# Attention and a ResMLP block on one core: constant rows on another DMA queue, merged casts of v, the sinks' product issued beside the scores, and a last tile in two column halves

## The chip, the cores and the metric

One NeuronCore of one Trainium2 chip. The metric is the device time of one execution in microseconds (us), as a median of several. TensorE (PE) does the matmuls and transposes, VectorE (DVE), ScalarE (ACT) and GpSimd (POOL) the work on elements, SyncE (SP) only issues DMAs; ScalarE and GpSimd can issue them too. "Granted clock" is the share of its full clock that TensorE was allowed. It is recorded for every run, as a mean over the run, and will turn out to matter here.

## The reference

```python
# q, k, v: (4, 8, 768, 64); n_sink = 4; window = 128
scores = q @ k.T / sqrt(64)
keep = (column < n_sink) | (0 <= row - column < window)
x = softmax(where(keep, scores, -1e9)) @ v       # -> (4, 768, 512)
tok = w_tok @ (alpha1 * x + beta1)               # mixes the 768 positions
u = x + lam * tok
a2 = alpha2 * u + beta2
out = u + lam * (relu(a2 @ w_ch1) @ w_ch2)       # w_ch1: (512, 2048)
```

## The kernel before

The kernel is written as tasks with a priority and a guessed cost. A list scheduler in Python, at build time, turns them into one order of instructions for each engine; the numbers in `TURNS` are seeds of small shuffles of the priorities that were found by trial. Where the scheduler expects TensorE to wait in the start, it puts in filler matmuls (a zero tile times itself, results unused):

```python
    def idle(pt, n):
        for _ in range(n):
            nc.tensor.matmul(pt[:, 0:P], warm, warm, start=True, stop=True)
    plan = Plan(pools, homes, (IDLE, idle, 75.0))
```

In `Plan.emit` they stand ahead of the task that the model expects to come late:

```python
        for t, e, start, stop, idle in self.run(prio):
            if idle:
                self.fill[1](... tile ..., idle[1])     # idle[1] fillers
            ...                                          # allocate buffers
            t.fn(e)                                      # emit the task
```

The three constant rows (lam, alpha1, beta1) are loaded by SyncE's queue into four partitions each, and spread by a shuffle on VectorE:

```python
    def load_row(p, name, tile_, src):
        done["row", name] = add(p, {SP: 500}, lambda e: nc.sync.dma_start(
            tile_.rearrange("(a i) d -> a i d", i=32)[:, 0, :],
            src.unsqueeze(0).to_broadcast([4, DM])), lands=(1, 100))
```

Attention of a tile r of 128 rows is one group of TensorE instructions: the sinks' part first, then the window's:

```python
    def pv(p, b, r, G):
        def mm(e):
            if r >= 2:      # the sinks' columns lie outside the window
                nc.tensor.matmul(po.t, es[b].t[g, (r - 2) * P : (r - 1) * P],
                                 vs[g, 4 * G : 4 * G + 4, :], start=True, stop=False)
            for hl in range(4):
                ...         # window: one or two matmuls a head
```

The result of the MLP of each tile is added and stored whole (512 columns), also in the last tile of all:

```python
                nc.vector.tensor_add(xf, xf, pc.t)
            ... nc.sync.dma_start(out[b, ti * P : (ti + 1) * P, :], ...)
```

The softmax here doesn't subtract the row's maximum and nothing guards it: scores larger than these inputs give would overflow.

## Time and profile before

| | before |
|---|---|
| median of the first 3 runs | 267.05 us (265.82 to 267.19) |
| span of the profiled run, with its time | 263.6 us, 265.35 us |
| first scores of batch 0 start | 13.25 us |
| first token-mixing matmul | 31.62 us |
| first unbroken run of MLP matmuls | 44.38 us |
| last add on VectorE starts | 259.80 us |

The prediction below shows the page's main lines, the waits, the chain and the timeline of the start. One view it does not show is TensorE in single microseconds of the start; one line of it suffices. Columns: stretch, its length, TensorE's busy time with the number of its matmuls, granted clock, DMA share, GB/s.

```profile
10.00:11.00 1.00, 0.00 (x0) 1.00 1.28 198
```

TensorE does nothing from 10 to 11 us: the fillers are in the wrong place, since the cast it waits for (1.62 us of waiting) comes later than the scheduler's model had it. In this run the clock stayed at 1.00. And this run, at 265.35 us, was faster than all three timed ones. Both facts deserved more attention than I gave them.

### The profile page before, as it was taken

The numbers are of one execution on the slowest core, as the hardware profiler recorded it, in microseconds if no ns is written. First come the engines' busy times: TensorE is split into PE (matmuls) and PEld (weight loads), VectorE is DVE, ScalarE is ACT, GpSimd is POOL, SyncE is SP. The second block draws the span as 40 slices with busy tenths as digits, with TensorE's granted clock in tenths as the row PEclk, the third lists the DMA queues.
The fourth block names the chain that finished last, engine by engine and source line by source line (L and its number), as shares of the span: only waits on it lengthen the run. The fifth ranks groups of instructions, "written<-read, shape, count | busy, mean of one in ns | idle before, by whom it ended". The sixth has DMA issues, their size and how long they took to land.

```text
span 263.6 us, 4930 instructions
## 1 busy us (share of the span) xinstructions
PE 254.4 (97%) x1947; PEld 140.3 (53%) x1947; DVE 156.0 (59%) x322; ACT 131.5 (50%) x216; POOL 81.6 (31%) x104
## 2 busy tenths in 40 slices
PE   8699997999999999999999999999999999999994
PEld 7555644765555545555655444556554445564441
DVE  3588996499899835288778327566962451100222
ACT  1499848788764123687740117877500226772000
POOL 8347936332830712333454212111131000000000
PEclk9999999999999999999999999999999999999999
DMA  7999999989937969999658979100012323000222
GB/s 132 195 241 308 295 268 269 371 229 270 210 64 174 221 144 211 183 214 209 120 126 140 249 147 196 44 0 2 1 42 80 80 80 82 0 0 2 80 81 80
DMA packets 85503, 38.49 MB, mean 146 GB/s; under 512 B 73428, under 2 KB 79580, under 8 KB 85480
## 3 DMA queue, kind: packets, MB, share of 16 engines
q1 hardware_dynamic: 81720, 34.90, 55.6%
q0 software_dynamic: 3744, 3.28, 7.9%
q8 instruction: 15, 0.25, 0.4%
q14 instruction: 8, 0.07, 0.1%
q10 hardware_dynamic: 16, 0.00, 0.0%
HBM read 29.65 MB, written 6.29 MB: 136 GB/s over the span
## 4 chain that ended last, share of the span: by engine, by line
PE 88%; DMA 9%; DVE 1%; ACT 0%; issue 0%; SPq 0%; DVEq 0%
PE h L971 32%; PE ch L995 32%; PE tok L891 9%; DMA nat<-in_k_dram 6%; PE S L689 4%; PE pv L773 4%; DMA nat<-in_q_dram 3%; PE S L684 1%; PE pv L766 1%; PE tp L595 1%; PE idle L342 1%; PE tp L592 1%; PE sk L637 1%; PE S_None L689 0%; PE uTp L932 0%; PE vsp_None L656 0%
## 5 line engine op out<-in xcount | busy, mean ns | idle before, releaser
L971 PE MATMUL h<-uT,w1f 128*128 128x384 f16 x512 | 89.3, 326 | 1.3 <-ACT uT L915 1.3
L995 PE MATMUL ch<-w2f,hT 128*128 128x512 f16 x384 | 88.8, 379 | 0.0
L971 PEld LDWEIGHTS <-w1f 128*128 128x128 f16 x512 | 48.3, 98 | 34.1 <-issue 3.6
L977 ACT ACTIVATE hT<-h 128x384 f16<-128x384 f32 x104 | 50.8, 491 | 26.5 <-PE h L971 26.1
L995 PEld LDWEIGHTS <-hT 128*128 128x128 f16 x384 | 36.0, 98 | 40.1 <-issue 0.4
L704 ACT ACTIVATE E<-S 128x1024 f16<-128x1024 f32 (+1 forms) x42 | 41.2, 1004 | 4.2 <-PE S L689 3.0
L1006 DVE TENSOR_TENSOR x<-x,ch 128x512 f32<-128x512 f32 x24 | 16.4, 686 | 44.0 <-PE ch L995 44.0
L813 POOL TENSOR_TENSOR xh<-x,la_b 128x512 f16<-128x512 f32 x18 | 25.3, 1410 | 51.5 <-DVE x L797 46.7
L349 ACT CAST u<-x 128x512 f16<-128x512 f32 x17 | 10.5, 617 | 53.8 <-DVE x L898 52.6
L891 PE MATMUL tok<-xh,wtokT 128*128 128x512 f16 x144 | 34.0, 379 | 0.3 <-DVE x L898 0.2
L898 DVE TENSOR_TENSOR x<-x,tok 128x512 f32<-128x512 f32 x24 | 16.3, 684 | 17.7 <-PE tok L891 17.7
L820 DVE SCALAR_TENSOR_TENSOR x<-lb_b,rsum,x 128x512 f32<-128x512 f32 x24 | 23.6, 1003 | 2.9 <-POOL xh L813 2.9
L891 PEld LDWEIGHTS <-wtokT 128*128 128x128 f16 x144 | 14.0, 98 | 16.8 <-issue 0.7
L351 POOL CAST vf<-vnat 128x512 f16<-128x512 f32 x18 | 12.9, 721 | 28.4 <-DMA vnat<-in_v_dram 17.9
L797 DVE TENSOR_TENSOR x<-pv,rec 128x256 f32<-128x256 f32 x48 | 20.4, 424 | 1.7
L979 DVE TENSOR_SCALAR hT<-h 128x384 f16<-128x384 f32 x24 | 13.2, 554 | 10.6 <-PE h L971 10.3
L773 PEld LDWEIGHTS <-E 128*128 128x128 f16 x328 | 15.3, 98 | 5.7 <-issue 1.4
L773 PE MATMUL pv<-vf,E 128*128 128x65 f16 x328 | 18.0, 194 | 0.0
L713 DVE TENSOR_TENSOR E<-E,maskn 128x1024 f16<-128x1024 f16 x25 | 18.0, 739 | 0.0
L351 POOL CAST n<-nat 128x768 f16<-128x768 f32 x14 | 12.4, 890 | 12.7 <-DMA nat<-in_k_dram 9.5
L351 POOL CAST u<-x 128x512 f16<-128x512 f32 x7 | 4.4, 628 | 33.9 <-DVE x L898 18.7
L689 PE MATMUL S<-qkT 64*128 64x256 f16 (+1 forms) x168 | 13.5, 270 | 0.0
(97 smaller groups left out, 198.1 us busy)
## 6 DMA issues: line engine op xcount, KB each, us to landing
out_dram<-x SPq DMA_DIRECT2D x24, 256.0 KB, 2.1
nat<-in_k_dram SPq DMA_DIRECT2D x13, 384.0 KB, 6.1
nat<-in_q_dram SPq DMA_DIRECT2D x13, 384.0 KB, 6.6
vnat<-in_v_dram SPq DMA_DIRECT2D x18, 256.0 KB, 4.6
wst_w<-in_moe_w_ch_dram SPq DMA_DIRECT2D x8, 512.0 KB, 9.1
wtn<-in_moe_w_tok_dram SPq DMA_DIRECT2D x6, 384.0 KB, 5.2
w1f<-in_moe_w_ch_dram POOLq DMA_DIRECT2D x4, 512.0 KB, 15.0
v<-in_v_dram SPq DMA_DIRECT2D x12, 128.0 KB, 7.6
```

Of the source, the lines that this page charges most:

```text
L351: engine[e].tensor_copy(o, i)
L689: nc.tensor.matmul(pv_[:, e_, i, :], o.t[rows, 2 * hp + 1, j * P : (j + 1) * P], o.t[rows, 2 * hp, j * P : j * P + w], start=not bias, sto ...
L704: nc.scalar.activation(eT.t, pS.t[:, :, 0 : n * w].rearrange("p e (i w) -> p e i w", i=n), AF.Exp, scale=scale)
L713: nc.vector.tensor_mul(ev, ev, m.to_broadcast(list(ev.shape)))
L773: nc.tensor.matmul(po.t[:, hl, :], eT.t[:, e_, off + i, c : c + P], vf[j][:, h, :], start=(r < 2 and n == 0), stop=(n == len(parts) - 1 an ...
L797: nc.vector.tensor_mul(bx.t[:, 4 * G : 4 * G + 4, :], po.t[:, :, 0:D], rec.t.to_broadcast([P, 4, D]))
L813: engine[e].tensor_mul(bh.t, bx.t.rearrange("p h d -> p (h d)"), la1_b)
L820: engine[e].scalar_tensor_tensor(out=xf, in0=lb1_b, scalar=rsum[:, r : r + 1], in1=xf, op0=ALU.mult, op1=ALU.add)
L891: nc.tensor.matmul(pt.t, wtokT[:, si, ti * P : (ti + 1) * P], hs[si].t, start=(si == 0), stop=(si == NR - 1))
L971: nc.tensor.matmul(ph.t, w1f[:, c, fi * P : (fi + 1) * P], bu.t[:, c, chk * NTOK : (chk + 1) * NTOK], start=(c == 0), stop=(c == NC - 1))
L977: nc.scalar.activation(bh.t[:, fi, :], ph.t, AF.Relu)
L995: nc.tensor.matmul(pc.t, bh.t[:, fi, nt * P : (nt + 1) * P], w2f[:, fi, :], start=(fi == 0), stop=(fi == NF - 1))
```

## The change

Its intent: let q and k arrive sooner, make fewer casts, use the array's row halves for the sinks' part of later tiles, and shorten the work after the last matmul. The diff, cut to its core (`TURNS`, the scheduler's constants and its start times also change, so the order of most instructions in the start does too):

```diff
+    for o_, src in ((lam_r, moe_lam), (la1_b, moe_alpha1), (lb1_b, moe_beta1)):
+        nc.scalar.dma_start(
+            o_.rearrange("(a i) d -> a i d", i=32)[:, 0, :], src.unsqueeze(0).to_broadcast([4, DM]))
-    for name, o, src in (("lam", ...), ("a1", ...), ("b1", ...)):
-        load_row(at(), name, o, src)
     def fold_rows():            # multiply first, then spread: one shuffle less
+        for name, key, o, p in (("a1", "la1", la1_b, -987), ("b1", "lb1b", lb1_b, -986)):
+            a = add(p, {DVE: 640, POOL: 1270}, lambda e, o=o: engine[e].tensor_mul(o, o, lam_r), ...)
+            done[key] = add(p + 0.5, {DVE: 640}, lambda e, o=o: nc.vector.stream_shuffle(o, o, [0] * 32), [a])
...
+    V0 = (((0, 1), (2, 3), (4, 5)), ((0, 1, 2), (3, 4, 5)))     # v casts of batch 0: 5, not 12
-    def cast_v0(p, G, r):
+    def cast_v0(p, G, rs):
...
+    EARLY = (2, 3, 4)
     def scores(...):             # of key tile j
+        r = j - 1
+        early = b > 1 and r in EARLY
         def mm(e):
+            for G in range(2) if early else ():
+                g = slice(64 * G, 64 * G + 64)       # row half G of the array
+                nc.tensor.matmul(pvb[b, r, G].t, es[b].t[g, (r - 2) * P : (r - 1) * P],
+                                 vs[g, 4 * G : 4 * G + 4, :], start=True, stop=False)
     def pv(p, b, r, G):
-            if r >= 2:
+            if r >= 2 and not early:
...
     def mlp2(p, b, ti, part):
+        if b == B - 1 and ti == NR - 1:
+            if part % 2 == 0:
+                mlp2_half(p, b, ti, part // 2)       # 16 matmuls of 256 columns, add, store
+            return
```

More of the change, by code (lines that the diff above doesn't have):

```diff
@@ L35 @@
 class Rings:
-    WIRE = {"hw": 1600.0, "sw": 1900.0}
+    WIRE = {"hw": 1600.0, "sw": 2100.0}
     HOLDS = 128.0
@@ L146, in run @@
                 b.left += 1
-        free = {e: 0.0 for e in (PE, ACT, DVE, POOL, SP)}
+        free = {PE: 0.0, ACT: 3500.0, DVE: 3200.0, POOL: 500.0, SP: 0.0}
         rings = Rings()
@@ L354 @@
     lam_b = const.tile([P, DM], FP32, name="lam_b")
+    lam_r = const.tile([P, DM], FP32, name="lam_r")
     la1_b = const.tile([P, DM], FP32, name="la1_b")
@@ L379 @@
     nc.vector.memset(sel, 0.0)
-    for o_ in (lam_b, la1_b, lb1_b):
+    for o_ in (lam_r, la1_b, lb1_b):
         nc.vector.memset(o_, 0.0)
+    for o_, src in ((lam_r, moe_lam), (la1_b, moe_alpha1), (lb1_b, moe_beta1)):
+        nc.scalar.dma_start(
+            o_.rearrange("(a i) d -> a i d", i=32)[:, 0, :], src.unsqueeze(0).to_broadcast([4, DM]))
     bias0 = const.tile([P, 1, 2 * P], FP16, name="bias0")
     biasn = const.tile([P, 1, 2 * P], FP16, name="biasn")
-    vf = []
+    vfs = const.tile([P, NR, H, D1], FP16, name="vfs")
     for r in range(NR):
-        t_ = const.tile([P, H, D1], FP16, name=f"vf{r}")
-        nc.vector.memset(t_[:, :, D : D + 1], 1.0)
-        vf.append(t_)
+        nc.vector.memset(vfs[:, r, :, D : D + 1], 1.0)
+    vf = [vfs[:, r] for r in range(NR)]
     bmf = bm.rearrange("p a e -> p (a e)").unsqueeze(2)
@@ L396 @@
     w2f = const.tile([P, NF, DM], FP16, name="w2f")
-    ROWS = 7500.0
+    ROWS = 7000.0
     PAIRS = 0
-    TURNS = (9001, 9014, 9033, 9144, 9184, 9189, 9257, 9267, 9317, 9319, 9376, 11442, 9006, 109010, 109011, 109029, 109037, 9153, 109163, 109208)
+    TURNS = (39286, 39315, 39323, 39754, 40467, 41250, 41382, 139002, 39003, 39015, 139040, 139062, 139089, 139154, 39159, 139160, 39171, 39387, 139559, 139625, 139757, 139905, 39966, 140019, 140036, 140073)
     W1_SINCE = 20000.0
+    V0 = (((0, 1), (2, 3), (4, 5)), ((0, 1, 2), (3, 4, 5)))
     XB = 2
@@ L479, in load_qk @@
             done["nat", b, hp, t] = add(
-                p, {POOL: 600}, lambda e: nc.gpsimd.dma_start(
+                p, {POOL: 740}, lambda e: nc.gpsimd.dma_start(
                     bf.t, src.rearrange("h (p r) d -> p h (r d)", p=P)), [wait], [bf], lands=(16, 76))
@@ L527, in load_wtok @@
             uses=[bf], lands=(8, 134))
-    def load_row(p, name, tile_, src):
-        done["row", name] = add(
-            p, {SP: 500}, lambda e: nc.sync.dma_start(
-                tile_.rearrange("(a i) d -> a i d", i=32)[:, 0, :],
-                src.unsqueeze(0).to_broadcast([4, DM])), lands=(1, 100))
     wst = {}
@@ L563 @@
     xn = {}
+    pvb = {}
+    EARLY = (2, 3, 4)
     def trans(p, b, hp, t, engs, evac, cast_p=None, wait=None):
@@ L676, in scores @@
         o = qkT[b]
-        def mm(e):
+        r = j - 1
+        early = b > 1 and r in EARLY
+        if early:
+            for G in range(2):
+                pvb[b, r, G] = Buf("d", [P, 4, D1], FP32, f"pv{b}_{r}_{G}")
+        def mm(e):
+            for G in range(2) if early else ():
+                g = slice(64 * G, 64 * G + 64)
+                nc.tensor.matmul(
+                    pvb[b, r, G].t, es[b].t[g, (r - 2) * P : (r - 1) * P], vs[g, 4 * G : 4 * G + 4, :],
+                    start=True, stop=False)
             for G, hps, n, pS, eT in units:
@@ L698, in scores @@
             p = p - 1000
-        a = add(p, {PE: cost}, mm, qk + [done["bias"]], [o] + [u[3] for u in units], mode="row")
+        more = []
+        if early:
+            cost += 115
+            qk = qk + [done["vs", b, None], done["es", b, 0]]
+            more = [es[b]] + [pvb[b, r, G] for G in range(2)]
+        a = add(p, {PE: cost}, mm, qk + [done["bias"]], [o] + [u[3] for u in units] + more, mode="row")
         for G, hps, n, pS, eT in units:
@@ L758, in pv @@
     def pv(p, b, r, G):
-        po = Buf("d", [P, 4, D1], FP32, f"pv{b}_{r}_{G}")
+        early = (b, r, G) in pvb
+        po = pvb[b, r, G] if early else Buf("d", [P, 4, D1], FP32, f"pv{b}_{r}_{G}")
         parts = [(r - 1, P)] * (r > 0) + [(r, 0)]
@@ L783, in pv @@
         uses = [po] + list(dict.fromkeys(eT for eT, _ in Es))
-        if r >= 2:
+        if early:
+            after.append(done["S", b, r + 1, 0 if r + 1 < NR - 1 else None])
+        elif r >= 2:
             after += [done["vs", b, None if b else G], done["es", b, G if b == 0 else 0]]
             uses.append(es[b])
-        a = add(p, {PE: (130, 245, 355)[min(r, 2)]}, mm, after, uses)
+        a = add(p, {PE: 245 if early else (130, 245, 355)[min(r, 2)]}, mm, after, uses)
         done["pv", b, r, G] = a
@@ L834, in cast_v @@
             p, {POOL: 645}, lambda e: copy(e, vf[r][:, :, 0:D], bf.t), [done["vn", b, r]] + prior, [bf])
-    def cast_v0(p, G, r):
-        bf, sl = v0["at", G, r]
-        done["vf", 0, r, G] = add(
-            p, {POOL: 400, ACT: 408, DVE: 330},
-            lambda e: copy(e, vf[r][:, 4 * G : 4 * G + 4, 0:D], bf.t[:, sl]), [done["v0", G, r]], [bf],
-            port=True)
+    def cast_v0(p, G, rs):
+        n = len(rs)
+        bf, sl = v0["at", G, rs[0]]
+        a = add(
+            p, {POOL: 190 + 215 * n, ACT: 195 + 213 * n, DVE: 215 + 115 * n},
+            lambda e: copy(
+                e, vfs[:, rs[0] : rs[0] + n, 4 * G : 4 * G + 4, 0:D], bf.t[:, sl : sl + n]),
+            [done["v0", G, r] for r in rs], [bf], port=True)
+        for r in rs:
+            done["vf", 0, r, G] = a
     def cast_wtok(p, ti):
@@ L984, in mlp1, with mlp2_half, mm, oa @@
         done["h", b, chk, fi] = add(p + 0.1, {ACT: 493, DVE: 556}, relu, [a], [ph, bh])
+    def mlp2_half(p, b, ti, half):
+        chk, nt = ti // 3, ti % 3
+        bh, bx = hT[b, chk], x[b, ti]
+        pc = Buf("d", [P, DM // 2], FP32, f"ch{b}_{ti}_{half}")
+        cols = slice(half * (DM // 2), (half + 1) * (DM // 2))
+        a = None
+        for part in range(2):
+            fis = range(8 * part, 8 * part + 8)
+            def mm(e, fis=fis):
+                for fi in fis:
+                    nc.tensor.matmul(
+                        pc.t, bh.t[:, fi, nt * P : (nt + 1) * P], w2f[:, fi, cols],
+                        start=(fi == 0), stop=(fi == NF - 1))
+            a = add(p + 0.5 * part, {PE: 8 * 108}, mm,
+                    [done["h", b, chk, fi] for fi in fis] + [done["w2", fi] for fi in fis] + [a], [pc, bh])
+        def oa(e):
+            xf = bx.t.rearrange("p h d -> p (h d)")[:, cols]
+            nc.vector.tensor_add(xf, xf, pc.t)
+        a = add(p + 0.6, {DVE: 380}, oa, [a, done["u16", b, ti]], [pc, bx])
+        add(p + 0.7, {SP: 480}, lambda e: nc.sync.dma_start(
+            out[b, ti * P : (ti + 1) * P, cols], bx.t.rearrange("p h d -> p (h d)")[:, cols]),
+            [a], [bx], lands=(8, 60))
     def mlp2(p, b, ti, part):
+        if b == B - 1 and ti == NR - 1:
+            if part % 2 == 0:
+                mlp2_half(p, b, ti, part // 2)
+            return
         chk, nt = ti // 3, ti % 3
@@ L1029 @@
         load_qk(at(), 0, hp, t)
-    for name, o, src in (("lam", lam_b, moe_lam), ("a1", la1_b, moe_alpha1), ("b1", lb1_b, moe_beta1)):
-        load_row(at(), name, o, src)
     for G in range(2):
@@ L1041, in fold_rows @@
     def fold_rows():
-        for name, o in (("lam", lam_b), ("a1", la1_b), ("b1", lb1_b)):
-            done[name] = add(
-                {"lam": -1895, "a1": -1894, "b1": -850}[name], {DVE: 640},
-                lambda e, o=o: nc.vector.stream_shuffle(o, o, [0] * 32), [done["row", name]])
-        done["la1"] = add(-880, {DVE: 640, POOL: 1270}, lambda e: engine[e].tensor_mul(la1_b, la1_b, lam_b),
-                          [done["lam"], done["a1"]], port=True)
-        done["lb1b"] = add(-825, {POOL: 1270, DVE: 640}, lambda e: engine[e].tensor_mul(lb1_b, lb1_b, lam_b),
-                           [done["lam"], done["b1"]], port=True)
+        for name, key, o, p in (("a1", "la1", la1_b, -987), ("b1", "lb1b", lb1_b, -986)):
+            a = add(p, {DVE: 640, POOL: 1270}, lambda e, o=o: engine[e].tensor_mul(o, o, lam_r),
+                    port=True, since=ROWS)
+            done[key] = add(p + 0.5, {DVE: 640}, lambda e, o=o: nc.vector.stream_shuffle(o, o, [0] * 32), [a])
         pt = Buf("d", [P, 2 * NC], FP32, "abT")
@@ L1060 @@
     for G in range(2):
-        for r in range(NR):
-            cast_v0(-900 + 60 * G + 10 * r, G, r)
+        for rs in V0[G]:
+            cast_v0(-900 + 60 * G + 10 * rs[0], G, rs)
     for G in range(2):
@@ L1103 @@
                 load_qk(t0 + 100 + i, 1, hp, t)
+            done["lam"] = add(
+                t0 + 150, {SP: 500}, lambda e: nc.sync.dma_start(
+                    lam_b, moe_lam.unsqueeze(0).to_broadcast([P, DM])), lands=(8, 90))
             for i in range(4):
```

## The prediction

> **What bounds the kernel now.** I read the page first, then the waits of TensorE, the chain of waits in order of time, the windows by stage, and the timeline of the first 15 us and of the end.
>
> ```profile
> PE 254.4 (97%) x1947; PEld 140.3 (53%) x1947; DVE 156.0 (59%) x322; ACT 131.5 (50%) x216; POOL 81.6 (31%) x104
> PEclk9999999999999999999999999999999999999999
> ```
>
> TensorE is busy for 97% of the span at full clock, but its busy time counts 97 filler matmuls, so the share alone says little. The waits of TensorE are more useful:
>
> ```profile
> PE tp L595 <- DVE n L351: 2.4, 2, 1.6
> PE h L971 <- ACT uT L915: 1.3, 2, 0.7
> PE idle L342 <- DVE warm L367: 1.1, 1, 1.1
> PE tok L891 <- DVE x L898: 0.2, 1, 0.2
> ```
>
> Nothing is in this list after 45 us. The windows (length, TensorE busy with its count, granted clock, DMA share, GB/s) show the same:
>
> ```profile
> 37.00:44.40 7.40, 5.60 (x42) 1.00 1.16 270
> 44.40:60.00 15.60, 15.60 (x133) 1.00 0.97 285
> 160.00:218.00 58.00, 58.00 (x415) 1.00 0.23 56
> 239.00:259.80 20.80, 20.69 (x96) 1.00 0.14 52
> ```
>
> So there are three parts: a start up to 44.4 us, in which batch 0's attention runs while data arrives; 215 us of gapless matmuls, whose length is their own work; and a tail. The chain shows what sets the early start:
>
> ```profile
> 2.89 0.50 DVE lb_b L382
> 3.39 0.16 SPq L532
> 3.55 0.06 issue
> 3.60 7.00 DMA nat<-in_q_dram
> 10.63 0.57 DVE n L351
> 11.25 0.51 PE tp L595 x6
> 44.38 2.27 PE h L971 x13
> 259.80 0.69 DVE x L1006
> ```
>
> A constant row (alpha1) sits in SyncE's queue between the first k and the first q, and must wait for VectorE's zeroing. The q behind it is issued at 3.60 instead of about 1.3 and lands 7.0 us later. On VectorE the same row does more harm:
>
> ```profile
> 2.87 0.68 SPq L532 DMA_DIRECT2D la_b<-in_moe_alpha_dram  x1
> 7.22 0.74 DVE L1045 STREAM_SHUFFLE la_b<-la_b 128x512 f32<-128x512 f32 x1
> 7.91 0.70 DVE L351 CAST n<-nat 128x768 f16<-128x768 f32 x1
> ```
>
> The k issued at 0.80 landed 3.0 us later, at 3.8; its cast ran only at 7.91, because the shuffle ahead of it waited for the row. From 10.6 on VectorE is the tight engine of the start (windows of four us: 3.93, 3.93, 3.29, 3.61 and 4.00 busy between 16 and 36 us), with ScalarE close.
>
> **What the Trainium skill says.** "DMA: Bandwidth & Descriptors", section "Issuing engines are not separate DMA queues": DMAs from all engines share the same 16 DMA engines, and another issuer saves only sequencer time. The trace agrees on the first half (DMA share 1.1 to 1.2 from 4 us on), but what is saved here is more than issue time: a wait of 2.1 us at the head of a queue that is served in order. "TensorEngine Tiling (Array Packing)", section "Tiling Modes": tiles work independently and changing the mode drains the array. The trace agrees: eight 64-row score matmuls of 256 columns take 0.54 us in the chain and four take 0.32 to 0.33, so four more cost 0.215: two row halves run together in the 0.11 of one full-array matmul of that width, and the 0.11 left over is the change of mode. "VectorE: DVE Perf Modes", section "Side-by-side: where the cycles go for N=2048 bf16", gives every instruction a fixed init of about 150 cycles; that is why fewer, longer casts should be cheaper. The cast of 128x256 took 309 ns on VectorE and 397 on GpSimd, the one of 128x512 about 600 to 720 on GpSimd, so most of a GpSimd cast is per element here.
>
> **The change part by part.**
> Rows. lam, alpha1 and beta1 go to ScalarE's queue, and alpha1 and beta1 are multiplied before they are spread, so one shuffle (0.73) goes; lam itself is later read as a 128-row broadcast, 256 KB instead of 8, in a stage where w2 is not yet needed. By the new order SyncE issues one v slice, then q, then k of the first pair, with no wait: q at about 1.3, k at 1.8. The first k landed in 3.0 us alone; two of 0.39 MB and a v slice of 0.13 behind one another, with the casting loads in parallel, I put at about 8 us (0.9 MB; the trace moved 106 GB/s to 4 us, 188 to 11). GpSimd's second casting load, needed for the first scores, becomes the second of its queue, not the third (third: issued 3.47, landed 7.3 later). A transpose fed by the third load now precedes the first scores. So they start at about 11.2, not 13.3: minus 2.
>
> VectorE in the start. From the eviction of the second k to the last normalization I count, at the durations of the trace: 3 evictions 2.9, masks 1.4, norms 12 x 0.56 = 6.7, three token-weight casts 3.1, two vs 0.8, row work 2.3, a fourth eviction's share and small ones 1.2: 18.4 us. The same stretch before holds 20.6 (four casts of v, 1.2, and a shuffle fall away) and ended at 32.0. If it begins at about 10 and idles 1 to 2 us as before, it ends at 29 to 30.5: minus 1.5 to 3.
>
> Token mixing. In the new order tiles 4 and 5 come after ten MLP groups instead of before, with their loads behind batch 1's q and k. That moves 2 x (6 x 0.216 + 0.33) = 3.2 us of TensorE work from the starved stage to the full one, and two more transposes (0.68) forward. It is no work saved, but the last tok, its add (0.69), cast (0.62) and eviction (2 x 0.68) leave gaps before the MLP of 2.8 us in all (between 37 and 44.4, from the chain and timeline), and the fillers differ. ScalarE now has two evictions and a cast (2.4 us) between the first cast of u and uT, so I expect 2.3 of these gaps to stay. Sum for the start: 2.3 from the VectorE stretch plus 0.5 here = 2.8.
>
> Sinks. Twelve full-array matmuls of 260 columns (0.11 each in the chain, batches 2 and 3) become six concurrent pairs beside the scores: 12 x 0.11 - 6 x 0.11 = 0.65 saved, all on the path, since TensorE has no gaps there. They hold two of the four accumulators longer, from the scores until the normalization; MLP groups then alternate between two. One group is 0.65 on TensorE; relu takes 0.49 plus 0.16 of waits, so two are just enough unless ScalarE is in an exponential (1.0). I take 0.4 back for that and for new joins in the order.
>
> Tail. Now: last matmul, add 0.69, store issued, 2.0 to landing, about 1.1 to the end. With two column halves the last add is 256 wide (0.42, as the normalization of that width); the store is half as large, say 0.2 less. 16 extra matmul issues cost under 0.1. Saved: 0.27 + 0.2 = 0.5.
>
> Sum: 2.8 + 0.65 - 0.4 + 0.5 = 3.55 us of 267.05: 263.5.
>
> **The rivals.**
> First, the start is bound by DMA (share above 1.1 from 4 to 48 us), so unblocking SyncE only moves the wait. For it: batch 1's second k landed 16.3 us after issue, and three of batch 1's transposes now stand before the uT transposes on TensorE. Against: 0.79 MB of token weights move behind them, nearly 3 us at 270 GB/s. If it holds, the start gains 1 instead of 2.8, and the time is about 265.3.
> Second, VectorE and ScalarE set the start wholly and the gaps before the MLP close with the new fillers: then the start gains about 4.5, and the time is 261.8 or a bit less.
> Third, the accumulators held by the early sinks, or late weights (the four w1 loads took 11 to 19 us to land, and the new order wants four parts within ten groups), put gaps of 1 to 2 us into the now gapless stretch: 265.
>
> **Range and chances.** The two safe parts (sinks, tail) give 1.1 us, 0.4%. The start is worth 1 to 4.5, stalls cost 0 to 1.5. Two per cent would be 5.3 us, below 261.7: this needs nearly everything of the second rival and no stall. Slower by 2% has no support. I predict 263.5, 8 in 10 between 261.3 and 265.6; faster 0.2, same 0.78, slower 0.02.
>
> **What would show it.** First scores at about 11 us, no shuffle ahead of the first casts, and the wait of TensorE for the cast of n shrunk: the row step. The last normalization of batch 0 at 29 to 30.5, and the first unbroken MLP group at about 39 (44.4 less 2.8, and less 3.2 - 0.7 of moved work). No waits of TensorE beyond 45: the accumulators suffice. The early sink pairs at 0.11 each, no longer a piece of their own before pv. Last add at about 0.42. It would be wrong if the first MLP group waits for a load (rival one), if uT is ready with no gap (rival two), or if waits for evictions appear between 120 and 200 us (rival three).

## The result, and the profile after

The changed kernel took 263.38 us (263.32 to 263.57, 4 runs); before, on the same chip, 267.12 (265.82 to 268.38, 4 runs). The ratio of the fast runs is 0.9862, 95% interval 0.9814 to 0.9909. Ratios here are the mean time of one kernel's fast runs over that of the other's of the same rounds, so they are not quite the ratios of the medians quoted. A run counts as slow, and is left out, when it is over 1.5% above the fastest of its kernel.

The waits of TensorE in the changed kernel (us in total, times, longest; the wait of the first fillers, 1.1 as before, is left out):

```profile
PE tp L594 <- DMA n<-in_k_dram: 0.6, 1, 0.6
PE uTp L957 <- POOL u L351: 0.6, 1, 0.6
PE h L996 <- DMA w1f<-in_moe_w_ch_dram: 0.6, 1, 0.6
PE tp L594 <- DMA n<-in_q_dram: 0.4, 1, 0.4
PE h L996 <- DVE uT L942: 0.3, 1, 0.3
```

The wait of the transposes for VectorE's cast of n, 2.4 us before, is gone; waits for loads (0.6 + 0.4) stand there. The waits ahead of the MLP were 1.3 + 0.2 and are now 0.6 (for u) + 0.3 (for uT), so they are 0.6 shorter; but a wait of 0.6 for w1 has come in behind them, at 50.5 us. The timeline of the changed kernel (start, duration, engine, line, operation, out<-in, count, idle before):

```profile
1.32 0.48 SPq L493 DMA_DIRECT2D nat<-in_q_dram  x1
1.85 0.47 SPq L493 DMA_DIRECT2D nat<-in_k_dram  x1
...
5.20 0.56 DVE L351 CAST n<-nat 128x768 f16<-128x768 f32 x1 [1.60 <-DMA nat<-in_q_dram]
6.61 0.84 DVE L351 CAST n<-nat 128x768 f16<-128x768 f32 x1 [0.85 <-DMA nat<-in_k_dram]
...
10.76 0.39 PE L702 MATMUL S<-qkT 64*128 64x256 f16 x4
...
39.31 1.46 PE L996 MATMUL h<-uT,w1f 128*128 128x384 f16 x7 [0.31 <-DVE uT L942]
...
47.15 2.75 PE L916 MATMUL tok<-xh,wtokT 128*128 128x512 f16 x12
50.47 2.12 PE L996 MATMUL h<-uT,w1f 128*128 128x384 f16 x12 [0.57 <-DMA w1f<-in_moe_w_ch_dram]
```

q and k are issued at 1.32 and 1.85, as expected. Both casts of the first pair are done by 7.5 us, where before the second ended at 11.2. Scores start at 10.76, not 13.25; MLP matmuls at 39.31, not 44.38. The last lines show where some of this lead ends: after the late token tiles TensorE waits for the last part of w1.

The stretch of VectorE that the prediction counts, from its first eviction to the last normalization of batch 0, in before and then in the changed kernel (stretch, length, VectorE's busy time with count, granted clock, DMA share, GB/s):

```profile
11.38:32.03 20.65, 17.72 (x52) 1.00 1.09 273
```

```profile
9.50:30.13 20.63, 17.17 (x46) 1.00 1.10 293
```

It starts 1.9 us sooner and is just as long as before: only 0.55 us of its work fell away (four casts of v went and one eviction came, among others), and VectorE idles that much more.

The sinks, in the chain of waits (start, us, what) of before and then of the changed kernel:

```profile
185.47 0.54 PE S L689 x8
186.02 0.22 PE pv L766
...
187.13 0.11 PE pv L766
```

```profile
185.75 0.22 PE pv L689 x2
185.96 0.44 PE S L702 x8
...
258.39 0.42 DVE x L1032
```

Before, a tile paid 0.54 for its scores and then two full-array sink matmuls, 0.22 with the change of mode and 0.11. Now two sink matmuls in row halves take 0.22 together with the change of mode, which the scores behind them no longer pay (0.44). Added up over the whole trace from the start of each TensorE record to the next, the sinks' matmuls cost 4.34 us before (32 of them) and 3.01 + 0.72 after (20 full, 12 in halves): 0.61 less. This count is of the sinks' matmuls alone. By the same count the window matmuls of pv behind 60 us rose from 8.18 to 8.70 us in the new order.

The last add now starts at 258.39, not 259.80: 1.41 sooner. It is 0.42 long, not 0.69, and the span is 1.9 shorter. So of these 1.9 us, 0.5 come after the last matmul. Where the other 1.4 were won shows in the work that is left: at 60.11 us in before and at 60.20 in the changed kernel the same matmuls remain, but for eight fewer of the MLP's first layer (428, not 436, at 0.164 us each). So the changed kernel is 1.2 us ahead there, which is the start's share; all that follows, the sinks included, adds 0.2. But the timed medians differ by 3.7. **The two profiled runs explain half of the gain.** The other half has to be in what distinguishes an ordinary run of before from its profiled one.

### What the runs of before look like

I put the 142 runs of the kernel before that the experiments brought along into classes of their mean granted clock, and did the same for the changed kernel and three near-identical variants of it (below: casts one by one, w2 held back, w1 sooner; all within 0.2 us in the median):

| mean granted clock | before: runs, median us | changed and three variants: runs, median us |
|---|---|---|
| 0.998 or more | 29, 264.55 | 25, 263.32 |
| 0.9945 to 0.998 | 4, 265.88 | none |
| 0.9895 to 0.9945 | 79, 267.19 | none |
| below 0.9895 | 30, 268.63 | none |

At the same full clock the kernels differ by only 1.2 us. Four fifths of before's runs are not at full clock. The first run below, the same kernel before, was profiled in such a state and shows where the clock goes.

Three cautions belong to this table. It pools three jobs on three chips (before's medians in them are 267.36, 266.42 and 266.44), and the changed kernel itself was run in the first comparison alone. 43 of the 142 runs of before count as slow, all of them below 0.9945, so a ratio of fast runs leaves out part of what a better clock is worth. And clock is not all that differs between the classes: they lie 2.6 and 4.1 us above the first, while one or two stretches of 3.4 us at half clock are 1.7 or 3.4 us of missing clock; and in the two runs with rows on ScalarE's queue below, 13 executions at 0.998 or more still took anything from 263.3 to 267.8 us.

### The profile page after: what moved, and what is told of

It is laid out like the page before. It is cut to its first block, busy times and chain, and to the rows that moved or that the text cites. A ratio compares the mean times of both kernels' runs of the same rounds, so it can differ in the third digit from the quotient of the medians.

```text
span 261.7 us, 4960 instructions
## 1 busy us (share of the span) xinstructions
PE 254.2 (97%) x1954; PEld 140.7 (54%) x1954; DVE 154.5 (59%) x315; ACT 134.3 (51%) x219; POOL 82.3 (31%) x100
## 4 chain that ended last, share of the span: by engine, by line
PE 82%; DMA 11%; POOL 3%; DVE 2%; issue 0%; POOLq 0%
PE ch L1052 31%; PE h L996 28%; PE tok L916 9%; DMA w1f<-in_moe_w_ch_dram 7%; PE pv L792 4%; PE S L702 4%; DMA n<-in_k_dram 4%; PE S L697 1%; PE ch L1023 1%; POOL n L486 1%; POOL xh L827 1%; PE pv L785 1%; DVE x L841 1%; DVE E L731 1%; PE sk L639 1%; DVE x L818 0%
## 5 line engine op out<-in xcount | busy, mean ns | idle before, releaser
L1052 PE MATMUL ch<-w2f,hT 128*128 128x512 f16 x368 | 86.5, 379 | 0.1
L1052 PEld LDWEIGHTS <-hT 128*128 128x128 f16 x368 | 34.4, 98 | 38.0 <-issue 1.0
L722 ACT ACTIVATE E<-S 128x1024 f16<-128x1024 f32 (+1 forms) x42 | 40.6, 1003 | 12.5 <-PE S L702 10.9
L841 DVE SCALAR_TENSOR_TENSOR x<-lb_b,rsum,x 128x512 f32<-128x512 f32 x24 | 21.9, 927 | 5.2 <-POOL xh L834 4.9
L1004 DVE TENSOR_SCALAR hT<-h 128x384 f16<-128x384 f32 x25 | 13.9, 555 | 17.8 <-PE h L996 17.2
L351 POOL CAST vfs<-vnat 128x512 f16<-128x512 f32 x18 | 13.3, 745 | 19.0 <-DMA vnat<-in_v_dram 12.3
L792 PE MATMUL pv<-vfs,E 128*128 128x65 f16 x328 | 17.8, 194 | 0.0
L351 POOL CAST u<-x 128x512 f16<-128x512 f32 x7 | 5.2, 743 | 38.0 <-DVE x L923 38.0
L351 POOL CAST n<-nat 128x768 f16<-128x768 f32 x12 | 10.6, 891 | 14.8 <-DMA nat<-in_q_dram 7.3
L349 ACT CAST n<-nat 128x768 f16<-128x768 f32 x12 | 9.9, 832 | 8.2 <-DMA nat<-in_k_dram 7.6
```

The lines of the kernel that those rows point to most:

```text
L349: nc.scalar.copy(o, i)
L351: engine[e].tensor_copy(o, i)
L722: nc.scalar.activation(eT.t, pS.t[:, :, 0 : n * w].rearrange("p e (i w) -> p e i w", i=n), AF.Exp, scale=scale)
L792: nc.tensor.matmul(po.t[:, hl, :], eT.t[:, e_, off + i, c : c + P], vf[j][:, h, :], start=(r < 2 and n == 0), stop=(n == len(parts) - 1 an ...
L841: engine[e].scalar_tensor_tensor(out=xf, in0=lb1_b, scalar=rsum[:, r : r + 1], in1=xf, op0=ALU.mult, op1=ALU.add)
L1052: nc.tensor.matmul(pc.t, bh.t[:, fi, nt * P : (nt + 1) * P], w2f[:, fi, :], start=(fi == 0), stop=(fi == NF - 1))
```

## The experiments

Three theories for the gain:
- **Loads and casts** (mine): q and k arrive sooner, so all of the start runs sooner.
- **Clock**: before leaves TensorE idle near 10 us, loses its full clock for some us after, in most of its runs; the changed kernel keeps TensorE busy there.
- **Shares of the other parts**: casts, sinks, tail, order of loads.

The first eight runs were designed for the first and third; the clock was found in their records. The last four test it, and the wait for w1.

### The kernel before again (no edit)

> The kernel before, unchanged, as its own test. The timed runs differed by 3.7 us between the kernels, the two profiles only by 1.9 (263.6 and 261.7 us of span). Theory A (chance in the one profile): its runs scatter over some 265.3 to 268.4 us and the profile of before caught a quick one. A second profile then has a span of 264 to 266.5, and the extra time lies in the start, before the first MLP group, as later landings of loads. Theory B (the profile is typical and the timed runs differ by something outside of the span): the span is 263.6 again while the times stay near 267.

267.78 us median (22 runs, 264.6 to 269.5), ratio 1.0027 [0.9997, 1.0056]. The profiled run, at 268.05 us and a mean clock of 0.991, shows in single microseconds:

```profile
10.00:11.00 1.00, 0.00 (x0) 1.00 1.28 197
11.00:12.00 1.00, 0.26 (x5) 1.00 1.27 192
12.00:13.00 1.00, 1.00 (x18) 0.61 1.27 195
13.00:14.00 1.00, 1.00 (x15) 0.50 1.27 226
14.00:15.00 1.00, 1.00 (x12) 0.50 1.12 239
15.00:16.00 1.00, 1.00 (x10) 0.68 0.75 165
```

The fifth number is the granted clock. After two idle microseconds it is one half from about 12.2 to 15.6 us: the missing shares, 0.39 + 0.50 + 0.50 + 0.32 = 1.71 us, are half of 3.4 us. The same group of 14 fillers is visibly slower, in this run and then in before's first profile:

```profile
13.15 1.67 PE L342 MATMUL idle<-warm 128*128 128x128 f16 x14
```

```profile
12.38 0.94 PE L342 MATMUL idle<-warm 128*128 128x128 f16 x14
```

The Trainium skill says in "TensorE: Matmul & The Clock Gate", section "What's actually happening", that the clock falls to half after an idle window of about 3.4 us, and that the windows run freely, so it varies from run to run where they fall. The length agrees, and so does the free running: in every trace here the recorded clock changes only at whole steps of 3.41 us from a first change that lies between 4.1 and 7.0 us. In this run one step was 8.81 to 12.22 us, with TensorE busy for 1.0 of it, and the half clock followed. In before's first profile the steps were 6.57 to 9.98 and 9.98 to 13.39; they cut the same idle time in two, each held 2.1 to 2.3 us of work, and nothing was lost. What does not agree is the word idle, as these busy times show (more in the last section).

Theory A holds for where the time lies: of the 2.7 us by which this span is longer, 2.1 are lost by the MLP's long run (46.47, not 44.38). Late loads are part of it: the Q tile's transposes are 0.5 late (11.74) before the clock falls, the scores behind them 1.5 (14.76), so about 1.0 came with the half clock. The last 0.65 is a wait for a relu on VectorE at 63.2 us, far behind the start.

### Rows on ScalarE's queue, in the kernel before

```diff
+    for o_, src in ((lam_b, moe_lam), (la1_b, moe_alpha1), (lb1_b, moe_beta1)):
+        nc.scalar.dma_start(o_.rearrange("(a i) d -> a i d", i=32)[:, 0, :], src.unsqueeze(0).to_broadcast([4, DM]))
-            (the DMA in load_row; its task stays, empty)
```

> The kernel before with its three rows issued from ScalarE's queue; the order of every other instruction is untouched. Row theory: q is issued at about 1.3 instead of 3.6 us and lands at 5 to 6, its cast no longer waits for it, but the shuffle of alpha1 still stands before the cast of k. First scores at about 12 instead of 13.3, time less by 0.5 to 1.2 us. Plan theory (the gain comes from the new order as a whole, the row is only a small part): less by under 0.5 us.

266.91 us median (22 runs, 263.3 to 269.8), ratio 0.9930 [0.9904, 0.9957]. The profiled run had its first scores at 12.25. The DMAs alone give some 0.7% in the fast runs and only 0.45 us in the median, for runs of all classes of clock remain (13 of 22 below 0.9945). The part alone is worth far less than taking it away costs in the changed kernel (next but one).

### The same, and alpha1's shuffle moved behind the first casts

```diff
+            nc.vector.stream_shuffle(la1_b, la1_b, [0] * 32)      # at the end of make_bias
-            (the shuffle at a1's old place)
```

> As the run before, and the shuffle of alpha1 comes behind the two casts and the two biases on VectorE. Row theory: both casts are done by about 6.5 us; the first scores then wait for the casting load of the second pair's k, which landed at 10.8, and start at 11.5 to 12; time less by 1 to 2 us against the kernel before. If VectorE's later queue or the loads bound the start all the same, the last normalization of batch 0 stays near 32 us and the time within 0.5 us of before.

266.24 us median (22 runs, 263.8 to 271.35), ratio 0.9978 [0.9952, 1.0005]: 1.1 us under before in the median, nothing sure by the fast runs. Its profiled run (clock 0.993) idled from 5.2 to 7.3 us, waiting for a load of n, and had half clock from 7.7 to 11.1 us, with first scores at 13.27. Clearing one wait uncovered a load's, and the clock gave the time back. Inconclusive on how much the shuffle was worth.

### Rows back on SyncE's queue, in the changed kernel

```diff
-        nc.scalar.dma_start(o_..., src...)            # all three rows
+        nc.sync.dma_start(o_..., src...)              # alpha1 between the first q and k, the others before v
```

> The changed kernel with the rows back on SyncE's queue: alpha1 between q and k, lam and beta1 behind the first v slices. Row theory: k is issued at about 3.5 instead of 1.85 us and lands at 9 to 10 instead of 6.6; the first scores of this order need it, so they start at 12 to 13 instead of 10.8, and the time is 0.5 to 2 us more than the changed kernel (264 to 265.4). If the loads bound the start (later casting loads landed at 12 to 14.2 us whatever SyncE does), it is within 0.4 us of the changed kernel (263.0 to 263.8).

267.29 us median (14 runs, 266.76 to 270.2), ratio 1.0004 [0.9972, 1.0036], clock 0.980 to 0.994 in all. Undoing this one part undoes the whole gain: 3.9 us over the changed kernel of the first comparison, and level with before of the same job. The timeline shows the K tile's transposes late, and what follows:

```profile
11.37 0.51 PE L604 MATMUL tp<-iden,n 128*128 128x128 f16 x6 [3.15 <-DVE n L351]
...
14.70 1.03 PE L704 MATMUL S<-biasn,iden 128*128 128x512 f16 x2
```

Transposes that ran at 8.39 in the changed kernel run at 11.37; two score matmuls of 512 columns take 1.03 us, not 0.60, at half clock. The first token-mixing matmul starts at 33.84, not 29.44. Either lateness or the clock could carry this; a run below separates them.

### The tail alone, in the kernel before

```diff
+    def mlp2_half(...)       # as in the change; used for the last tile alone
```

> The kernel before with the last tile in two column halves and nothing else: less by 0.5 us (0.27 from the add, 0.2 from the smaller store), so the last add at about 0.42 and the end 3.3 us after its start instead of 3.8. If the store's time does not depend on its size, 0.25.

266.61 us median (22 runs, 263.0 to 270.9), ratio 0.9951 [0.9915, 0.9988]. In the highest class of clock it is 264.19 (8 runs) against 264.62 for before in the same job (10 runs): 0.4 us, near the 0.5 of the two traces. The medians of all runs (266.61 against 266.42) cannot resolve it: one lost stretch of clock is four times as large.

### The sinks back in pv, in the changed kernel

```diff
-            for G in range(2) if early else ():
+            for G in ():
...
-            if r >= 2 and not early:
+            if r >= 2:
```

> The changed kernel with the sinks' share of batches 2 and 3 as full-array matmuls in front of their pv again, in the changed order, with the accumulators held as long. If TensorE's own work sets the middle, it is longer by 12 x 0.11 - 6 x 0.12 = 0.6 us: 264.0. If the pairs only fill time in which TensorE waited for exponentials or relus, it is the same within 0.2 us.

263.88 us median (8 runs, 263.5 to 264.4), ratio 0.9917: 0.5 us over the changed kernel of the first comparison (263.38), 0.6 to 0.7 over the two variants of the same job that follow. So in this order the sinks' part is worth 0.5 to 0.7, with 0.61 counted in the trace.

### The casts of v one by one, in the changed kernel

```diff
-            lambda e: copy(e, vfs[:, rs[0] : rs[0] + n, 4 * G : 4 * G + 4, 0:D], bf.t[:, sl : sl + n]),
+            lambda e: [copy(e, vfs[:, r, 4 * G : 4 * G + 4, 0:D], bf.t[:, sl + i]) for i, r in enumerate(rs)],
```

> The changed kernel with v of batch 0 cast tile by tile, on the same engines and at the same places of their queues: GpSimd 6 x 0.40 instead of 3 x 0.6 to 0.77 and 3 x 0.40 instead of 0.83, ScalarE 3 x 0.41 instead of 0.84. Per-instruction theory: ScalarE loses 0.4, GpSimd 0.5 to 0.9 us in the start, of which 0 to 0.5 us reaches the end. If casts lie beside other work: within 0.2 us of the changed kernel. In either case the old kernel's four casts on VectorE (1.1 us) are not tested by this.

263.22 us median (6 runs, 262.7 to 264.8), ratio 0.9892. No effect: the merged casts are not on the path.

### An early load of w2 held back, in the changed kernel

```diff
+        if key == "w2_10":
+            held.append(f)        # issued with the next w2 load
+            return
```

> The changed kernel with its first load of w2 (0.5 MB, issued at 18.5 us, first needed after 70) moved behind batch 1's q and k. Load theory of the start: the loads behind it land up to 1.9 us earlier (0.52 MB at 275 GB/s), the wait for the last part of w1 at 50 us (0.57, with 0.7 of gap) shrinks, and the time is less by 0.4 to 1.2 us: 262.2 to 263.0. If the start is bound by VectorE and by the order before uT alone: less by under 0.3.

263.28 us median (6 runs, 262.9 to 264.25), ratio 0.9881. No effect on the time. In its profile, of the slowest of its runs (264.25 us), the wait for w1 is 1.8 us, not 0.6: the held load does not hurry w1. I take back the idea that contention of this load with w1 costs anything.

### The fourth w1 load right behind the third, in the changed kernel

```diff
+        steps = self.run(prio)
+        at = {getattr(s[0], "w1", None): n for n, s in enumerate(steps)}
+        steps.insert(at[2] + 1, steps.pop(at[3]))
```

> The kernel after with the fourth load of w1 issued right behind the third on GpSimd, ahead of two folds of xh (1.4 us sooner, the folds 0.8 us later). In after TensorE waits 0.57 us for this part of w1 at 50.5 us. If that wait is where some of the start's gain went, 262.7 to 263.2 us; if the next wait takes its place, or the later folds cost as much, the same as after, 263.2 to 263.7.

263.39 us median (9 runs, 262.9 to 264.4), ratio 0.9898: the same as the changed kernel. Its timeline at the place in question:

```profile
46.65 2.75 PE L920 MATMUL tok<-xh,wtokT 128*128 128x512 f16 x12
50.32 2.12 PE L1000 MATMUL h<-uT,w1f 128*128 128x384 f16 x12 [0.92 <-DMA w1f<-in_moe_w_ch_dram]
```

TensorE came to this place 0.50 us sooner than in the changed kernel (46.65, not 47.15), and w1 only 0.15 sooner (50.32, not 50.47), so the wait grew by 0.35, to 0.92. Here one sees a lead being given back: what is won ahead of this load ends at its arrival. It was also my last attempt at a version better than the changed kernel; none of the twelve beats it clear of noise.

### More fillers, in the kernel before

```diff
+            n_more = {(0, 0, 1): 12, (0, 0, 0): 26}.get(getattr(t, "pre", None), 0)
+            if n_more:            # ahead of the first two late transposes of batch 0
+                self.fill[1](... the tile of that task ..., n_more)
```

> The kernel before with 38 more filler matmuls (a zero tile, results unused) ahead of the first two batch-0 transposes that wait for VectorE: 12 ahead of the K tile's (8.67 us in the profile of before) and 26 ahead of the Q tile's (11.25 us); 0.056 us each, so they end at about 8.6 and 11.1 us and fit in the idle stretches. Order, transfers and every other instruction are as before; first scores stay at about 13.2 us. Clock theory (half of what before loses is a stretch of some 3.4 us at half clock that follows TensorE's idle time at 9.6 to 11.2 us, in most of its runs): granted clock of 0.998 or more in most runs, median 264.2 to 265.0 us, 2 to 3 us under before of the same job. Rival, the chain of loads and casts (the gain is time by which work ahead of the MLP starts sooner): no earlier start, so the same as before within 0.5 us, and the clock scatters as it does in before.

265.30 us median (22 runs, 264.43 to 267.67); before in the same job 266.44 (46 runs, 263.66 to 271.71). The clock did what the theory says: 20 of 22 runs have 0.9945 or more, of before 16 of 46, and none of the runs counts as slow, of before 16 do. The median is 1.1 us lower, not 2 to 3, and by the fast runs alone nothing is shown: ratio 0.9994 [0.9968, 1.0020]. At full clock these runs take 265.34, and before's at full clock 264.47 in this job. Either 38 fillers cost 0.9 us in a way that I did not find (the first scores came at 13.41, 0.16 later), or before's full-clock runs are a lucky choice, those whose loads came early and so left TensorE less idle. The expectation of 264.2 to 265.0 failed.

### No fillers after the first group, in the changed kernel

```diff
-            if idle:
+            if idle and not self.filled:
+                self.filled = True
```

> The kernel after with only its first group of filler matmuls (those that warm the clock up to 5.8 us); the 43 later ones (14, 11, 4, 2, 2, 9, 1) are left out. They stand only in time in which TensorE waits, so the work is as early as in after: first scores at about 10.8 us. Clock theory: with TensorE idle for about half of 6.2 to 10.3 us, some or most runs lose a stretch at half clock: clock 0.993 in these, median 264.5 to 266 us, 1 to 2.5 us above after's 263.4. Rival (chain of loads): same as after within 0.3 us, 263.1 to 263.7.

264.48 us median (22 runs, 262.56 to 266.97; 21 of them count as fast), ratio 0.9976 [0.9948, 1.0004]. 20 of 22 runs are below 0.9945; of the changed kernel and its variants none of 25. Nothing but results that nobody reads was taken out, and it costs 1.1 us in the median (264.48 against 263.39 for the w1 variant of the same job), or 0.8%, 2.1 us, by the ratios (0.9976 over 0.9898). From its profile, single microseconds again:

```profile
10.00:11.00 1.00, 0.16 (x6) 1.00 1.28 191
...
12.00:13.00 1.00, 1.00 (x8) 0.57 1.29 193
13.00:14.00 1.00, 1.00 (x16) 0.50 1.26 224
```

The half clock comes as in before, although TensorE was busy for two thirds of the stretch from 8 to 12 us. In the changed kernel the clock is 1.00 throughout. The runs of this kernel give the price of the clock without a second kernel: 262.56 at 0.998 or more (2 runs), 263.93 at 0.9895 to 0.9945 (6 runs), 265.20 below (14 runs), so about 1.3 us for each stretch of half clock. The first scores came at 11.30, not 10.8, behind a load, so the work was not quite as early in the profiled run. The two runs that kept the clock are 0.8 under the changed kernel: again as if fillers cost something, again too few runs and perhaps lucky ones.

### Rows back and the idle stretch filled, in the changed kernel

```diff
+            n_more = {(0, 0, 1): 50}.get(getattr(t, "pre", None), 0)     # on top of "rows back"
```

> The run in which after's rows went back to SyncE's queue (267.3 us, clock 0.993 or less, TensorE idle from 7.9 to 11.4 us) with 50 more fillers in that idle stretch. Clock theory: clock 0.998 or more, and what stays is only the lateness of the K tile: 264.0 to 265.5 us. Rival (the lateness of K is what cost 3.9 us): 266.8 to 267.8 us still.

268.67 us median (6 runs, 268.07 to 270.76), ratio 1.0129 [1.0073, 1.0184]. The clock theory asked for 264.0 to 265.5 and failed here outright. The fillers did hold the clock at 1.00 up to 20 us, and the K transposes were at 11.36, as they were without them. But then (single microseconds):

```profile
20.00:21.00 1.00, 0.44 (x8) 1.00 1.08 197
...
23.00:24.00 1.00, 1.00 (x11) 0.51 1.01 346
```

A second sparse stretch, in which TensorE waits for VectorE, cost the clock there instead. And the one run that kept it, at 0.998 or more, took 268.07. So I put most of the 3.9 us of "rows back" down to the lateness of K in an order tuned for an early K. This is argued, not shown: one run alone kept its clock, 50 fillers more make another kernel, and in the first 16 us the kept clock did gain 0.9 (the same score matmuls at 14.74, not 15.66), which the second stretch then lost.

## Why the prediction was right or wrong

The time (263.38 for 263.5) came out, and so did the mechanism of the rows, the sinks and the tail. VectorE's part did not, and the sum came out by luck: the start's term was too large, and a cause that I had not seen filled the place.

**Rows and VectorE.** First scores at 10.76 (I said 11.2), no shuffle ahead of the casts, the wait for the cast of n gone, the last normalization of batch 0 ended at about 30.1 (29 to 30.5; before 32.0). MLP matmuls began at 39.31 (39). The row step was right, and "rows back" shows that it rests on where the rows are issued. The end of VectorE's stretch was right for another reason than mine. I set 18.4 us of work against 20.6 before; but 20.6 is the length of that stretch before, which held 17.7 us of work. It did not get shorter (20.63, not 20.65), it began at 9.50 instead of 11.38. Two readings were also too broad: the DMA share was 0.97 to 1.07 from 16 to 28 us, not above 1.1 throughout, and VectorE was busy for only 2.31 of the 4 us from 12 to 16, so it was not yet the tight engine.

**The start's worth, "2.3 from the VectorE stretch plus 0.5 here = 2.8", is the step that failed.** In the two profiles, at full clock on both sides, it was 1.2, the lead at 60 us. Token mixing began 2.18 sooner, but 12 transposes of token weights (0.68) had only moved from ahead of it to behind it, so 1.5 of that was real. The 0.5 for smaller gaps ahead of the MLP came too (waits of 0.9, not 1.5), but the new wait of 0.57 for w1, which was in my third rival, took it back; the w1 variant shows that it swallows leads. For the 0.3 that then still lack I have only scattered small stalls and no experiment.

**The missing cause.** My first reading was "TensorE is busy for 97% of the span at full clock". It was true of the profiled run and not of three in four of before's runs, whose mean clock fits one or two stretches of 3.4 us at half clock. Part of the change's gain is that its order and its fillers keep TensorE busy from 8 to 12 us (3.6 of the 4 us, against 1.7 in before's profile). Taking the changed kernel's fillers away costs 1.1 us in the median (2.1 by the ratios), and putting some into before gains 1.1 in the median, though nothing in the fast runs alone; within the runs without fillers one stretch costs 1.3. So I estimate this share as 1 to 2 us. That fillers hold the clock, and that removing them costs time, is shown; the exact share is not.

**Sinks.** I said 0.65 less 0.4 for joins and held accumulators. The trace has 0.61 for the sinks' matmuls, the experiment 0.5 to 0.7, and no waits for accumulators appear in the list. But the 0.4 for joins was needed: all that lies between 60 us and the last add gained 0.2, near the 0.25 that I had summed.

**Tail.** 0.5 predicted; 0.5 in the traces, 0.4 by the full-clock runs of the experiment.

**The sum.** For the medians, 3.7 in the first comparison and 3.0 to 3.2 in the two later jobs that had near-identical variants: tail 0.4 to 0.5, all else behind 60 us 0.2, clock 1 to 2, and what is left, 0.3 to 2.1, holds the 1.2 that the start shows in the profiles. It closes no tighter than that: in the classes at full clock the kernels differ by 1.2 in all, in the two profiles by 1.9. I had put 2.8 into the start, by work moved forward alone; the clock made up what it lacked, and that is the luck. The rivals: the DMA-bound start (a gain of 1) was close in number for the moved work; the one in which all gaps close fell.

**Open.** Why runs with added fillers are 0.8 to 0.9 us slower at the same granted clock than those without (in both directions), and how the lateness of loads and the clock divide before's scatter: its runs at low clock may also be those whose loads came late. And the new order of instructions as such (`TURNS`, token tiles 4 and 5 later) was never run without the other parts, so it stands untested as a rival or a helper of the rows.

## What to carry to other kernels

Read the granted clock of every timed run, not of the profiled one alone: here three of four runs of a "tuned" kernel missed 1.7 us of clock or more in a stretch that its only profile did not show, and a change of 1.4% was, by my estimate, in good part a change of which clock the runs got. A stretch on an engine has a length and a content: set work against work, and ask whether it got shorter or only began sooner. Where TensorE must wait for data early in a kernel, fillers should cover the wait as it is measured, and it pays to test them by taking them out. And work that is moved ahead is worth only what survives the next late arrival; look for that load before counting the lead.

## What the Trainium skill lacked or had wrong

- "TensorE: Matmul & The Clock Gate", section "What's actually happening", names an idle window of about 3.4 us as what halves the clock. The length of the loss agrees (1.71 us of missing clock in 12 to 16 us, half of 3.4). But the window need not be idle: the six that were followed by half clock in these traces had TensorE busy for 1.0 to 2.0 of 3.41 us (2.0 in the run without fillers), while one of 1.8 in that same run was not. So no limit can be read off here, and elsewhere the page speaks only of frequent short idle times, without a figure. Transposes are not the explanation, though the section "Part 4: PE-mode transpose" says that they do not count as busy in the same way: the window from 19.61 to 23.03 in the last run held 1.7 us of work and not one transpose, and half clock followed.
- The same section gives the penalty of the ramp as below 1% of a typical kernel's span, for the warm-up. A window lost later comes on top of that: each is about 1.7 us of clock in 265, 0.65%, and 30 of 142 runs of before have a mean clock below 0.9895 and a median 4.1 us, 1.5%, above those at full clock (not all of it clock). The section says that the number of slow matmuls varies from run to run; that this can decide a comparison of 1% is what no page says.
- "DMA: Bandwidth & Descriptors", section "Issuing engines are not separate DMA queues", says that another issuer saves only sequencer time. Three small rows put back on SyncE's queue, where one waits for VectorE's zeroing with the first k behind it, cost 3.9 us of 263.4, with the clock that these runs lost. What a blocked head does to the DMAs behind it belongs on that page. (A DMA share of 1.1 to 1.2, which the prediction gives as agreement, shows that the 16 engines are busy; that the issuers share them, no run here tests.)
- "VectorE: DVE Perf Modes", section "Side-by-side: where the cycles go for N=2048 bf16": the fixed start of each instruction is not disputed, but casts in twos and threes in place of single ones changed nothing (263.22 against 263.38 us): they were off the path, and they ran on GpSimd and ScalarE, of which that section does not speak.
